# A searched issue order replaced by another from pair 12 on, in a kernel of clustered attention and a causal expert layer

## The chip, the cores and the metric

One core of one Trainium2 chip runs the whole program in one launch. The metric is the device time of one execution in microseconds, given as the median of several runs; smaller is better. Engines are called PE (TensorE), DVE (VectorE), ACT (ScalarE), POOL (GpSimd) and SP (SyncE, which here only issues transfers).

## The reference

Two parts follow each other. Clustered attention: 4 batches of 8 heads, 768 positions, head size 64; every q and k row is assigned to the nearest of 16 centroids of its head, and a query sees only the keys of its own cluster. The result, heads side by side, is the input of an expert layer: 4 experts, each with causal attention of its own (head size 64), of which every position uses two, weighted by its gate.

```python
mask = q_assign[:, :, :, None] == k_assign[:, :, None, :]
scores = np.where(mask, scale * np.matmul(q, k.transpose(0, 1, 3, 2)), -1000000000.0)
attn = softmax(scores)                      # rows, with 1e-9 in the divisor
x = (attn @ v).transpose(0, 2, 1, 3).reshape(B, S, H * D)
logits = x @ w_gate                         # the two largest of 4, softmax over them: w
for e in range(E):
    a = softmax(causal(scale * (x @ wq[e]) @ (x @ wk[e]).T))
    out += (chosen e) * w * (a @ (x @ wv[e]) @ wo[e])
```

## The kernel before, in words

Work goes in head pairs, since two heads of 64 fill the 128 partitions. Pairs 0 to 15 are the clustered attention, pairs 16 to 23 the experts (four batches, two pairs of experts each). The function `core(n)` does a pair's attention, in two halves of 384 queries. It makes the scores twice: once with queries on the partitions, to find each row's maximum (L873 for attention, L877 for the experts; DVE masks and reduces at L886 and L888), and once with keys on the partitions (L960), with the maximum subtracted by additional contraction rows, so that ACT can apply the exponential (L966) straight into `p`. The row maxima travel to those rows `tk` by a small SBUF transfer from `tm`. POOL sets the causal zeros (L971). L1004 multiplies `p` with the values.

The divisors are sums over keys. The exponentials are first added up across key blocks into `acc` (helper `sum_op`: L326 on POOL or L327 on DVE), and one visit of PE, `total` (L1044), sums over the partitions. The sums go through `ssb` (L1048 on ACT or L1051 on DVE), to DRAM (`sd`), back in another layout (`r`, L1067 takes the reciprocal; with the gate's weights `g` at L1069), to DRAM again (`rd`) and back as a broadcast (`rb`), with which the product is normalised (L1095 for attention, an L326 or L327 into `avu` for the experts, followed by a split into a rounded part, `xk` or `kt`, and its rest, `xq` or `qt`). The last pair does without that way through DRAM: `last_half` sums with one-column matmuls (L790, L792) and broadcasts with small ones (L805).

The experts' q and k projections are L666 and L675, their values L706, the gate L712 to L755, the output projection L1133: three matmuls for every 128 rows and every pair, whose result ACT or DVE copies out of PSUM for the transfer to `out_dram`. A transfer is always issued by SP, in the order in which SP meets it (helper `dma`, L311), and a waiting transfer holds up those behind it.

No program order sets what is issued when. The code builds a `Plan` of 2499 steps, and each step may hold several instructions. Two tables written out in the file replay a search that was made beforehand: `ORDER` lists the steps as they are issued (`34` is step 34; a `*` makes it take its other engine, as ACT or DVE for a copy and POOL or DVE for an addition; `~8` puts in 8 filler matmuls), and `SLOTS` gives the slot of each buffer, among them 642 uses of the four double banks of PSUM (`pp`). `Plan.run` checks that no step comes ahead of one that it needs, and then calls them in turn. An instruction waits on the chip only for what it needs and for the former users of its slots.

```python
for step in ORDER.split():
    ...
    other = step[-1] == "*"
    o = self.ops[int(step.rstrip("*"))]
    ...
    list(o.ways.values())[other][1]()
```

Of the kernel before, what the change touches and what calls it, by code (L numbers as in the profile page):

```python
# [35 lines left out]
0 19 ~34 1 4 2 31 ~7 5 8 7 56 6 11* 9 3 10 32 12 ~17 20 13* 16* 33 21 55 22 54 35 34 ~13 60 14 147 39 18* 23 61 17* 24  # L36
62* 15* ~21 25 148 29 28* 41* 27 30* ~8 70 74 71 68 36 75 80 38 242 72 69 37 78 73 57 79 59 76 58 87 77 63 93 335 85
40 81 94 82 42* 88 83 44 84 86 64 91 241 105 92 100 106 45 114 101 46 108 115 102 109 47 95 103 111 96 104 89 112 117
90 97 66* 98 150 99 243 107 430 48 49 118 121 51 52* 110 53 244 162 50 133 122 163 336 158 134 113 119 159 160 120 127
161 156 116 128 166 43 157 130 167 124 131 123 164 125 136 165 146 168 169 65* 338 170 137 138 561 126 188 145 139 152  # L40
129 177 186 189 140 178 171 187 191 132 172 141 175 200 192 176 142 173 201 135 197 174 179 198 181 144 180 194 190
143 182 195 203 183 154* 184 149 185 151 193 655 196 222 204 213 258 223 537 254 259 219 205 199 255 260 547 220 216
261 560 252 153* 217 214 253 250 215 256 251 225 218 257 228 226 548 275 229 262 231 276 221 245 263 246 232 264 233
224 67 206 234 227 337 294 240 155 271 235 295 202 282 272 236 269 265 283 237 285 230 266 429 280 286 270 288 281
247* 273 289 291 274 267 292 239 207 284 297 268 238 277 278 248* 279 431 432 748 287 308 307 290 298* 367 309 354 368
536 310 538 355 350 311 293 319 208 351 299 352 320 313 353 312 348 314 209 346 349 316 347 344 317 315 322 345 323
325 356 357 318 326 358 327 211 535 300 328 321 550 329 374 334* 296 330 361 388 375 331 362 359 551 389 210 376 360
654 363 324 377 379 364 365 380 369 366 382 340 370 385 332 339 342* 333 301 383 562 386 391 371 372 378 563 373 302
341 437 381 402 401 392* 444 403 384 413 303 445 438 414 416 439 842 541 440 387 417 404 441 448 405 446 449 410 390
447 442 411 407 443 406 408 419 450 451 420 452 305 421 409 393 422 412 423 470 249 428* 461 656 471 482 304 462 459  # L50
483 468 415 394 460 424 479 306 469 425 463 473 480 549 418 464 457 474 453 458 476 434 472 454 455 427 477 485 426
456 475 465 466 395 467 436* 936 478 498 486 495* 579 499 577 580 496 396 481 749 578 594 497 507 595 543 573 508 484
501 574 539 575 502 569 576 397 510 500 570 571 511 504 487 572 433 503 505 513 581 582 514 552 583 515 540* 506 488
516 399 517 599 343 522* 509 518 590 607 600 591 584 608 542* 604 585 519 398 586 605 489 601 587 512 588 602 592 589
613 565 521 593 610 603 490 520 611 596 597 614 616 598 567 545 751 606 564 843 657 435 609 638 617 212 626 673 491
639 665 544* 674 629 612 666 669 1031 630 627 670 671 628 632 672 554 663 631 633 667 664 641 668 635 642 492 684 636
675 644 634 658 645 659 676 646 615 677 493 647 637 685 701 648 698 702 653* 640 680 699 693 681 649 678 695 694 679
650 643 688 618 696 686 689 707 566* 687 682 651 704 619 683 652 705 697 690 845 708 710 691 750 692 660* 620 568 700
721 711 720 759 722 621 661* 723 760 937 761 724 729 762 763 725 730 726 764 757 727 767 1030 758 703 735 768 765 736
# [12 lines left out]
1028 1062 1056 524 1063 1075 1086 905 1027 1035 1057 942* 1066 1067 1068 1076* 906 1037* 1087 1154 1139 1096 1155 1088  # L72
1102 526 1140 1133 1079 1103 1097 1132 1134 1135 1098 1099 1136 559* 1143 1100 1082 1111 1144 998 1141 1112 1158 1142
1108 523 1101 1159 1137 1109 1105 1138 1085 1106 1114 1145 1146 1115 1147 1104 1116 1117 1107 1118 1174 1123 944 1127
553* 1177 1175 1000 1168 1178 1110* 1156 1119 1163 1169 1157 1113 1120 1171 1164 1150 1148 1172 1151 1165 1036* 1129
1121 1149 1152 1122 1166 1180 1153 999 1160 1161 1167 1126 1162 1219 555* 1170* 1190 1229 1173 1181 1233 1230 1193
1234 1566 1235 1194 1191 1089 1131* 1236 1218 1227 1192 1196 1228 1237 1195 1197 1231 1202 1232 1199 1203 1238 1176
1205 1567 1239 1240 1200 1241 1198 1128 1206 1208 1221 1209 1223 1090 1179 1210 1091 529 1182 1201 1211 1092 1259 1217
1038 1262 533* 1260 1212 1204 1248 1263 1271 1249 1242 1272 1268 1207 1243 1213 1252 1257 1269 1253 1214 1130* 1246
1001 1258 1250 1247 1265 1251 1244 1215 1266 1261 1274 1216 1245 1183 1220 1093 1254 1222 1255 1094 1256 1568 1312  # L80
1264* 1284 1321 1275 1336 1267 1322 1296 1337 1323 1297 1285 1276 1324 1270 1327 1286 1313 1287 1184 1328 1329 1288
1290 1225* 1330 1325 1291 1331 1326 1293 1185 1289 1332 1342 1294 1299 1333 1300 1302 1292* 1334 1295 1343 1335 1303
1304 1186 1224* 1362 1311 1305 1320 1273 1346 1363 1351 1306 1347 1338 1298 1352 1353 1277 1339 1307 1359 907 1354
# [5 lines left out]
1432 1577 1440 1433 1453 1582* 1318* 1434 1579* 1435 1580 1583 1443 1370 1446 1466 1454 1463 1455 1483 1467 1475 1449
1484 1095 1493 1283 1476 1464 1494 1456 1319* 1491 1572 1465 1478 1492 1485 1479 1469 1486 1468 1487 1470 1472 1488  # L90
1489 1473 1504 1471* 1500 1592 1490 1474 1495 1496 1590 1505 1497 1452 1587 1371 1593 1372 1501 1373 1584 1374 1481
1588 1591 1589 1585* 1586 1625 1515 1626 1521 1516 1482* 1498 1522 1513 1499 1506 1514 1524 1507 1508 1517 1525 1518
# [1117 lines left out]
```

## Time and profile before

| | |
|---|---|
| median of 3 runs | 647.41 us |
| the runs | 646.45, 647.41, 649.11 us |
| span of the profiled execution | 644.0 us |
| its own time | not recorded apart; the median is 3.4 us above the span |
| mean granted clock of PE | 0.997 of full |
| PE busy | 634.8 us, 99% |
| DVE, POOL, ACT busy | 484.6, 466.9, 302.5 us |

The span runs from the first to the last instruction of the profiled execution; the time of a run also holds what lies before and after it. A PE that is busy all the time is the bound whatever the others do, so the table by stretch, the chain and the timelines of single engines are what tells a change of order apart.

### The profile page before, as it was taken

To read this page: it belongs to the slowest core of one execution; us is meant where nothing else is said; L and a number is where in the kernel's file an instruction comes from. 1 tells how busy PE (TensorE), PEld (TensorE's weight loads), DVE (VectorE), ACT (ScalarE), POOL (GpSimd) and SP (SyncE) were. 2 spreads that over 40 slices of the span, in tenths; PEclk is the share of its full clock that TensorE was granted. 3 is DMA by queue.
4 is the path that set the end of the run, shared out by engine and by line. 5 is a ranking of instruction groups with operands and counts; after the bars stand their busy time and mean duration, and the time that the engine had idled before them with its cause. 6 is when DMAs were issued, how large, how long until landed. Compare 5 with 4: busy or idle time off the path is not lost.

```text
span 644.0 us, 13775 instructions
## 1 busy us (share of the span) xinstructions
PE 634.8 (99%) x5404; PEld 482.6 (75%) x5404; DVE 484.6 (75%) x813; ACT 302.5 (47%) x499; POOL 466.9 (72%) x337
## 2 busy tenths in 40 slices
PE   8999999999999999999999999999999999999997
PEld 7667677676776666767757787879879879878775
DVE  5987888798787786888989656574885696678843
ACT  4756546466464654646556323342342423244523
POOL 4399999999999999999999937763754476122500
PEclk9999999999999999999999999999999999999989
DMA  9654445445253323425542310311321220021223
GB/s 192 106 93 95 112 97 113 102 101 106 56 121 99 93 60 86 128 70 107 119 125 75 102 57 2 99 52 51 100 75 28 75 78 24 21 83 68 85 93 131
DMA packets 128119, 55.99 MB, mean 87 GB/s; under 512 B 109820, under 2 KB 117688, under 8 KB 128056
## 3 DMA queue, kind: packets, MB, share of 16 engines
q1 hardware_dynamic: 126488, 54.74, 33.8%
q8 instruction: 42, 0.69, 0.5%
q10 hardware_dynamic: 1568, 0.39, 0.3%
q14 instruction: 21, 0.17, 0.1%
HBM read 39.29 MB, written 15.67 MB: 85 GB/s over the span
## 4 chain that ended last, share of the span: by engine, by line
PE 79%; POOL 14%; issue 2%; DVE 2%; ACT 1%; DMA 0%; SPq 0%; POOLq 0%; ACTq 0%; DVEq 0%
PE pp L960 22%; PE pp L1004 20%; PE pp L666 11%; POOL acc L326 10%; PE pp L873 7%; PE pp L1133 6%; PE pp L706 5%; PE pp L1044 2%; PE pp L877 2%; POOL xt L1095 2%; DVE mx L888 1%; PE pp L522 1%; POOL tk L326 1%; PE pp L1148 1%; POOL tq L326 1%
## 5 line engine op out<-in xcount | busy, mean ns | idle before, releaser
L326 POOL TENSOR_TENSOR acc<-acc,p 128x768 f32<-128x768 f32 (+2 forms) x143 | 249.2, 1752 | 42.0 <-DVE acc L327 38.0
L888 DVE TENSOR_REDUCE mx<-pp 128x2 f32<-128x768 f32 (+1 forms) x224 | 204.2, 943 | 47.8 <-PE pp L873 37.1
L966 ACT ACTIVATE p<-pp 128x768 f32<-128x768 f32 (+2 forms) x264 | 196.8, 773 | 78.4 <-PE pp L960 71.6
L960 PE MATMUL pp<-tq,tk 64*128 64x384 f32 (+2 forms) x1584 | 180.1, 333 | 0.8 <-ACT p L966 0.6
L960 PEld LDWEIGHTS pp<-tq,tk 64*128 64x128 f32 x1584 | 135.7, 186 | 20.7 <-issue 11.9
L1004 PE MATMUL pp<-p,vt 128*64 128x384 f32 x768 | 130.9, 491 | 0.0
L1004 PEld LDWEIGHTS pp<-p,vt 128*64 128x64 f32 x768 | 52.4, 137 | 75.9 <-issue 69.0
L326 POOL TENSOR_TENSOR acc<-p,p 128x768 f32<-128x768 f32 (+1 forms) x41 | 74.3, 1813 | 19.8 <-ACT p L966 18.0
L960 PE MATMUL pp<-tk 49*128 49x384 f32 (+2 forms) x528 | 88.3, 329 | 0.0
L873 PE MATMUL pp<-tk,tq 64*128 64x384 f32 x384 | 69.9, 360 | 1.0 <-ACT ssb L1048 0.7
L873 PE MATMUL pp<-tk 48*128 48x384 f32 x384 | 65.7, 338 | 0.0
L971 POOL TENSOR_SCALAR_AFFINE_SELECT p<-p 128x256 f32<-128x256 f32 x48 | 20.5, 443 | 54.6 <-ACT p L966 53.9
L873 PEld LDWEIGHTS pp<-tk,tq 64*128 64x128 f32 x384 | 48.4, 248 | 6.8 <-issue 2.1
L960 PEld LDWEIGHTS pp<-tk 49*128 49x128 f32 x528 | 50.3, 185 | 0.0
L873 PEld LDWEIGHTS pp<-tk 48*128 48x128 f32 x384 | 49.1, 252 | 0.1
L321 ACT ACTIVATE avu<-pp 128x384 f32<-128x384 f32 x32 | 15.7, 490 | 70.9 <-PE pp L1004 57.1
L886 DVE TENSOR_TENSOR pp<-pp,tri 128x256 f32<-128x256 f32 x48 | 20.6, 428 | 26.5 <-PE pp L877 23.1
L1004 PE MATMUL pp<-p,vm 128*64 128x384 f32 (+2 forms) x288 | 39.6, 420 | 0.0
L1095 POOL TENSOR_TENSOR xt<-avu,rb 128x384 f32<-128x384 f32 x24 | 29.7, 1277 | 11.0 <-DMA rb<-rd 11.0
L1004 PEld LDWEIGHTS pp<-p,vm 128*64 128x64 f32 x288 | 19.3, 137 | 22.6 <-issue 17.9
L327 DVE TENSOR_TENSOR acc<-acc,p 128x768 f32<-128x768 f32 (+2 forms) x23 | 24.7, 1072 | 7.5 <-POOL acc L326 7.5
L706 PE MATMUL pp<-wvh,xh 128*128 128x260 f32 x96 | 27.5, 287 | 0.0
(212 smaller groups left out, 993.5 us busy)
## 6 DMA issues: line engine op xcount, KB each, us to landing
rb<-rd SPq DMA_DIRECT2D x46, 192.0 KB
x<-xt SPq DMA_DIRECT2D x16, 384.0 KB
out_dram<-xt SPq DMA_DIRECT2D x21, 256.0 KB
vt<-in_v_dram SPq DMA_DIRECT2D x52, 96.0 KB
vt<-x SPq DMA_DIRECT2D x12, 384.0 KB
kt<-in_k_dram SPq DMA_DIRECT2D x28, 96.0 KB
qt<-in_q_dram SPq DMA_DIRECT2D x28, 96.0 KB
rw<-rows SPq DMA_DIRECT2D x14, 192.0 KB
```

What stands on the lines that cost most here:

```text
L326: ways = [("pool", t_pool(n), lambda: POOL.tensor_tensor(dst(), a(), b(), op=fn)), ("dve", t_dve(n), lambda: DVE.tensor_tensor(dst(), a(), ...
L327: ("dve", t_dve(n), lambda: DVE.tensor_tensor(dst(), a(), b(), op=fn))]
L666: PE.matmul(m()[:, hf, :HW], w_[:, dc, es], x_[dc]()[:, c], start=(i == 0), stop=(i == 3 * DC - 1))
L706: PE.matmul(m()[:, c % 2, :NV], x_[dc]()[:, ts], w_[:, dc, :], start=(i == 0), stop=(i == 3 * DC - 1))
L873: PE.matmul(ps()[:, h, :HW], at, kt[rs, i * HW:(i + 1) * HW], start=(j == 0), stop=(j == 1))
L886: DVE.tensor_tensor(e, e, tri[:, None, :].to_broadcast([128, 2, 128]), op=OP.add)
L888: DVE.tensor_reduce(to, ps()[:, :, :w], axis=AX.X, op=OP.max)
L960: PE.matmul(to, kt[rs, kc * 128:(kc + 1) * 128], by, start=(i == 0), stop=(i == 3))
L966: ACT.activation(pt()[:, :, o_:HW], p()[:, :, o_:HW], AF.Exp, scale=SC)
L1004: PE.matmul(av()[h * 64:(h + 1) * 64, 0, o_:HW], d["vv"](h, kc), pt()[:, h, o_:HW], start=(kc == 0), stop=(kc == nk - 1), tile_position=(0 ...
L1095: e.tensor_tensor(xt().rearrange("d (j u f c) -> d f c u j", j=32, u=4, f=2)[:, par], avu()[:, c].rearrange("d (c u j) -> d c u j", c=HC, ...
L1133: PE.matmul(m()[:, c % 2], a_()[:, ts], w_()[:, ep, :], start=(ep == 0 and i == 0), stop=(ep == EP - 1 and i == 2))
```

## The change

Only the tables `ORDER` and `SLOTS` are replaced. The plan's steps, their code and their instructions stay as they are; a step may take its other engine.

```diff
@@ -33,121 +33,121 @@
 ORDER = """
-0 19 ~34 1 4 2 31 ~7 5 8 7 56 6 11* 9 3 10 32 12 ~17 20 13* 16* 33 21 55 22 54 35 34 ~13 60 14 147 39 18* 23 61 17* 24
...
+4 19 0 ~34 1 2 31 ~7 5 8 56 7 6 11* 9 3 10 32 12 13* ~17 20 16* 21 55 54 22 33 147 ~13 60 23 35 34 14 24 39 18* 62*
...
 SLOTS = """
-0123131012302132213130202120103332000331312211201122200333130300321312110023102221312303203310223022110220033031211331
...
+0123131002302032213131202021113332010331332211200012121333032200313221320012301113231202102320133011230110033032122312
...
```

The table's first lines differ as well, but there only steps of different engines stand in another order among each other, which no engine sees: every engine keeps its rows up to about 322.7 us of the trace, the second half of pair 12. Behind it 109 steps take their other engine: 36 additions or subtractions go from POOL to DVE and 22 from DVE to POOL, one product of L1095 goes from DVE to POOL, 23 copies go from ACT to DVE and 23 from DVE to ACT, and four more steps (`ssb` among them), two each way. POOL has 13 instructions fewer, DVE 13 more. PE has the same matmuls in another order. Of the 642 uses of PSUM banks 439 have another slot, also in the half whose order is the same, and some 60 buffers in SBUF have.

SP's queue at the place where the orders part, around 320 to 326 us. `rd`, `rb`, `r` and `sd` belong to the divisors, `vt` is loaded values, `x` and `vm` the expert layer's input, and `tk` from `tm` the row maxima of pair 13. Before:

```order
L311 DMA rd<-r_4416 128x12
L311 DMA tk_95<-tm_4591 1x4x96 x2
L311 DMA rb_4602<-rd 64x768 x2
L311 DMA vt_4619<-in_v_dram 32x2x384 x4
L311 DMA r_4661<-sd 128x12
L311 DMA x_107<-xt_3773 128x768
```

After:

```order
L311 DMA rd<-r_4416 128x12
L311 DMA vm_4550<-x_103 128x768
L311 DMA x_107<-xt_3757 128x768
L311 DMA r_4572<-sd 128x12
L311 DMA rb_4595<-rd 64x768 x2
L311 DMA tk_95<-tm_4602 1x4x96 x2
```

The maxima's transfer has moved from behind `rd` to behind `rd`, two moves of `x`, `r` and `rb`.

The divisors of pair 22, near 609 to 623 us. On ACT before, where `xk` is the rounded part of the pair ahead and `p` are exponentials:

```order
L321 ACTIVATE xk_8193<-avu_7714 128x768
L966 ACTIVATE p_0_8195<-pp_8127 128x2x256
L1048 ACTIVATE ssb_8204<-pp_8175,eps 128x384
L966 ACTIVATE p_0_8206<-pp_8149 128x768
L743 ACTIVATE gs_7901<-gs_7901 128x6
L321 ACTIVATE avu_8221<-pp_8175 128x384
```

On DVE after:

```order
L327 TENSOR_TENSOR avu_7693<-avu_7693,rb_8085 128x768
L322 CAST xk_8195<-avu_7693 128x768
L327 TENSOR_TENSOR xq_8211<-avu_7693,xk_8195 128x768
L327 TENSOR_TENSOR acc_0_8213<-p_0_8193,p_0_8209 128x768
L1051 TENSOR_SCALAR ssb_8218<-pp_8197 128x384
L322 COPY avu_8220<-pp_8197 128x384
L327 TENSOR_TENSOR acc_0_8213<-acc_0_8213,p_0_8186 128x768
```

`ssb` has gone from ACT (L1048) to DVE (L1051), and now follows the normalisation of the pair ahead.

SP's queue for the same pair, with the gate's transfers `gd` and `g` and the outputs between. Before:

```order
L311 DMA sd<-ssb_8204 4x384
L311 DMA out_dram<-xt_8230 128x512
L311 DMA r_8249<-sd 128x12
L311 DMA gd_8251<-gr_8245 24x128
L311 DMA out_dram<-xt_8247 128x512
L311 DMA g_8265<-gd_8251 128x12
L311 DMA rd<-r_8249 128x12
L311 DMA out_dram<-xt_8282 128x512
L311 DMA out_dram<-xt_8296 128x512
L311 DMA rb_8304<-rd 64x768 x2
```

After:

```order
L311 DMA sd<-ssb_8218 4x384
L311 DMA out_dram<-xt_8230 128x512
L311 DMA gd_8241<-gr_8236 24x128
L311 DMA out_dram<-xt_8251 128x512
L311 DMA r_8254<-sd 128x12
L311 DMA g_8257<-gd_8241 128x12
L311 DMA g_8268<-gd_8241 128x12
L311 DMA rd<-r_8254 128x12
L311 DMA out_dram<-xt_8287 128x512
L311 DMA rb_8302<-rd 64x768 x2
```

The read of `r` has moved behind `gd` and a second output; `rb` stands at the same distance from `sd`.

PE near the end, from 620.7 us on: the last pair's one-column sums and the output projection (`s` and `rows` are the slots that hold the two parts of the weights). Before:

```order
L790 MATMUL pp_8291<-ones_85,acc_0_8191 128x1
L792 MATMUL pp_8291<-ones_85,p_0_8270 128x1
L790 MATMUL pp_8291<-ones_85,acc_0_8191 128x1
L792 MATMUL pp_8291<-ones_85,p_0_8270 128x1
L790 MATMUL pp_8298<-ones_85,acc_0_8189 128x1
L792 MATMUL pp_8298<-ones_85,p_0_8122 128x1
L790 MATMUL pp_8298<-ones_85,acc_0_8189 128x1
L792 MATMUL pp_8298<-ones_85,p_0_8122 128x1
L790 MATMUL pp_8298<-ones_85,acc_0_8189 128x1 x2
L790 MATMUL pp_8291<-ones_85,acc_0_8191 128x1 x4
L1133 MATMUL pp_8313<-s_5460,kt_8098 128x512
L1133 MATMUL pp_8313<-rows_5467,kt_8098 128x512
```

After:

```order
L790 MATMUL pp_8280<-ones_85,acc_0_8233 128x1
L792 MATMUL pp_8280<-ones_85,p_0_8183 128x1
L790 MATMUL pp_8280<-ones_85,acc_0_8233 128x1
L792 MATMUL pp_8280<-ones_85,p_0_8183 128x1
L790 MATMUL pp_8292<-ones_85,acc_0_8213 128x1
L792 MATMUL pp_8292<-ones_85,p_0_8270 128x1
L790 MATMUL pp_8292<-ones_85,acc_0_8213 128x1
L792 MATMUL pp_8292<-ones_85,p_0_8270 128x1
L1133 MATMUL pp_8189<-s_5092,kt_8073 128x512
L1133 MATMUL pp_8189<-rows_5461,kt_8073 128x512
L1133 MATMUL pp_8189<-s_5092,qt_8082 128x512
L790 MATMUL pp_8280<-ones_85,acc_0_8233 128x1 x2
```

The L1133 group stands ahead of the last one-column matmuls now, which follow in three pieces, each behind three L1133.

## Rows read from the trace of the kernel before

**Rows 1.** The page's busy line: busy us, share, instructions of each engine

```profile
PE 634.8 (99%) x5404; PEld 482.6 (75%) x5404; DVE 484.6 (75%) x813; ACT 302.5 (47%) x499; POOL 466.9 (72%) x337
```

**Rows 2.** Stretches: length, busy us per engine (PE, PEld, DVE, ACT, POOL), PEclk, DMA, GB/s

```profile
317.00:644.00 327.00, 323.08 (x2604) 261.23 (x2604) 225.62 (x426) 126.45 (x243) 174.64 (x151) 0.99 0.23 72
620.00:623.00 3.00, 3.00 (x25) 2.55 (x23) 1.76 (x3) 0.00 (x1) 0.00 (x0) 1.00 0.39 137
624.00:627.00 3.00, 3.00 (x10) 2.42 (x10) 0.52 (x3) 0.00 (x0) 0.00 (x0) 0.50 0.30 94
```

**Rows 3.** The chain that ended last, behind 322: start us, us, work

```profile
323.58 4.02 PE pp L1004 x24
327.61 0.90 PE pp L960 x8
...
412.13 2.31 PE pp L666 x12
...
439.74 2.10 PE pp L666 x12
...
631.63 8.56 PE pp L1133 x36
640.25 0.60 ACT xt L321
```

**Rows 4.** Timeline of PE, 606 to 644: start us, length, engine, line, operands

```profile
609.67 0.85 PE L1044 MATMUL pp<-acc,ones 128*32 128x384 f32 x8
...
620.71 0.35 PE L790 MATMUL pp<-ones,acc 128*128 128x1 f32 x2
...
622.48 1.65 PE L790 MATMUL pp<-ones,acc 128*128 128x1 f32 x12
623.99 0.78 PE L1133 MATMUL pp<-s,kt 128*128 128x512 f32 x1
...
626.70 0.68 PE L790 MATMUL pp<-ones,acc 128*128 128x1 f32 x4
627.24 0.48 PE L1133 MATMUL pp<-s,xk 128*128 128x512 f32 x1
...
631.56 0.50 PE L1133 MATMUL pp<-s,kt 128*128 128x512 f32 x1
```

**Rows 5.** Timeline of the other engines and SP's queue, 612 to 632

```profile
612.07 0.58 ACT L1048 ACTIVATE ssb<-pp,eps 128x384 f32<-128x384 f32 x1
...
615.35 0.38 SPq L311 DMA_DIRECT2D r<-sd  x1
...
622.22 1.10 SPq L311 DMA_DIRECT2D rb<-rd  x2
...
627.92 0.95 DVE L327 TENSOR_TENSOR avu<-avu,rb 128x768 f32<-128x768 f32 x1
...
629.50 0.96 DVE L327 TENSOR_TENSOR qt<-avu,kt 128x768 fp32r<-128x768 f32 x1
```

**Rows 6.** Timeline at the seam: the row maxima of pair 13

```profile
323.87 0.44 DVE L923 STREAM_TRANSPOSE tm<-M 128x192 f32<-128x192 f32 x1
...
324.34 1.16 SPq L311 DMA_DIRECT2D tk<-tm  x2
...
325.60 1.17 SPq L311 DMA_DIRECT2D rb<-rd  x2
```

**Rows 7.** Additions into acc by engine: ns min/median/max, first and last start

```profile
L327 DVE TENSOR_TENSOR acc<-acc,p x23: 414/957/2496, 233.1 to 619.9; 128x768 f32<-128x768 f32 x18, 128x512 f32<-128x512 f32 x3, 128x256 f32<-128x256 f32 x2
L326 POOL TENSOR_TENSOR acc<-acc,p x143: 727/1842/2548, 33.5 to 607.5; 128x768 f32<-128x768 f32 x126, 128x256 f32<-128x256 f32 x12, 128x512 f32<-128x512 f32 x5
```

**Rows 8.** Timeline around 313: an addition beside two POOL products

```profile
312.24 3.52 POOL L1095 TENSOR_TENSOR xt<-avu,rb 128x384 f32<-128x384 f32 x2
...
313.01 1.76 DVE L327 TENSOR_TENSOR acc<-acc,p 128x768 f32<-128x768 f32 x1
```

**Rows 9.** Timeline around 607: the last addition of POOL into acc

```profile
607.49 0.73 POOL L326 TENSOR_TENSOR acc<-acc,p 128x256 f32<-128x256 f32 x1 [3.86 <-DVE acc L327]
```

More of the change, by code (lines that the diff above doesn't have):

```diff
@@ L89 @@
[L89 to L92, printed above, removed]
-1509 1527 1519 1376* 1502 1528 1633 1600 1503 1477 1510 1511 1692 1601 1573* 1512 1480* 1634 1574* 1695 1520 1457 1458
@@ new lines @@
+732 766 752 728 769 753 770 771 733 738 739 740 706 494 712 741 731 747 801 742 772 709 743 787 773 802 744 782 622
+788 774 734 789 775 795 790 783 745 792 746 796 737 713 776 793 778 777 798 755* 780 779 799 804 781 791 784 785 939
+786 938 623 714 624 805 815 794 625 814 859 715 816 817 860 855 818 754* 820 856 861 821 716 851 862 829 556 797 558
+853 852 806 830 826 400 854 823 827 819 857 824 832 858 800 863 864 833 865 834 822 662 835 803 883 841* 874 836 884
+889 825 875 837 872 866 890 873 838 881 756 717 867 892 882 886 893 828 868 839 887 870 807 869 895 847 840 831 876
@@ new lines @@
+1451 1436 1424 1562* 1438 1437 1421 1439 1431 1422 1444 1401 1392 1429 1317 1402 1581 1445 1319 1281 1430 1395 1404
+1578 1403 1432 1433 1316* 1453 1579 1573 1580 1582 1434 1372 1583 1373 1318 1435 1440* 1443* 1374 1454 1463* 1466 1320
+1504 1467 1475 1505 1487 1476 1478 1455 1488 1506 1479 1464 1507 1489 1465 1472 1490 1468 1483 1473 1469 1484 1491
+1470 1493 1575* 1485 1471 1494 1584 1446* 1587 1486 1449 1492 1592 1376* 1375 1577 1377 1590 1456 1691 1474 1481 1593
+1588 1585 1589 1591 1495 1477 1496 1586 1497 1480 1482 1635 1508 1636 1500 1515 1452 1501 1524 1516 1509 1513 1525
@@ new lines @@
+1965 1967 1962 2077 1980 1983 1978 1968* 2070 2074 2064 2075 2160 1997 1961 2071 1986* 1989 2154 2161 2162 2065 2157
+2155 2066 2078 1990* 2067 2039 2156 1902 1969 1994* 1898 2158* 2151 2159 1874 1899 2152* 2231* 1903 2153 2232* 1999
+1900 2234* 1904 1905 2239 2040 1901 2235* 2000 2177 2084 2178 1966 2236 2089 2081 2079 2090 2085 2080 2179 2171 2082
+1910 2172 1970 2083 1906 2086 2088 1998 2240 1911 2180 1907 2241* 2167 1908 2110 2168 1912 1909 2107 2111 1913 2117
+2087* 2108 2163 2105 2041 2118 2237* 2121 2164 2106 2238* 2113 2122 2114 2091 2093 2109* 2115 2119 2094 2104* 2175
@@ new lines @@
+2173 2092 2165 2174 2095 2242 2176 2042 2245 2043 2044 2045 2046 2047 2048 2049 2050 2051 1914 2243 2052 2181 2166
+1918 2262 2182 2112* 2183 1971 2169 2116 1915 2244 2170 2246* 1919 2247 2254 2096 2123 1916* 2120 1920* 2264 2124 2251
+2097 1972 2098 2053 2099 2260 2252* 2253 2100 2054 2258 2248 2261 2259 2055 2256 2056 2249 2101* 2057 2263 1973 2250
+2125 2257 2058 2265 2102* 2255 1921 1917 2266 2103 1974 2126 2192 2187 2193 2299 2220 2188 2300 2184 2189 2221 2267
+2289 2216 2268 2185 2290 1975* 2224 2217 2297 2208 2298 2225 2210 2218 2209 2194 2213 2186 2211 2190 2291 2293 2214
@@ L150 @@
-123
+0101010101010110101000000000000000000000000011000110010111110101010101010011010100110110101000101000000000000000010321
+032
 """
```

180 lines of the change are left out of this document (82 added, 98 removed), and 6 rows, old and new, of the table ORDER.

## The prediction

> **What bounds the kernel now.** I read the busy line of the page first [rows 1]: in a span of 644.0 us TensorE is busy 634.8, the other engines at most three quarters. A mean hides stages, so the table by stretch came next, cut where the two programs begin to differ. In the 327 us behind 317 [rows 2] PE is busy 323.1; the missing 3.9 us are the end of the program, where the chain shows the last matmuls ending at 640.2, then one eviction and the output transfer [rows 3]. So from 317 to 640 TensorE never stands, while DVE works 225.6 and POOL 174.6 of the 327 us. The chain that ended last says the same: from 323 on it is a string of PE lines. The reader is to see that only two things can move the end: PE's own matmuls taking another time, or another engine, slack before, now making PE wait.
>
> One stretch of PE is slower than the rest. From 624 to 627 the granted clock is 0.50, which is 1.2 GHz, where 620 to 623 has 1.00 [rows 2]. Ahead of it stands an unbroken run of one-column matmuls, the sums of the last pair (L790, L792), from 620.71 to 623.99; the L1133 matmuls that follow take half as long again, until 627.24 [rows 4].
>
> **The change, part by part.** Up to about 322.7 us (second half of pair 12) every engine keeps its rows. Behind it the same matmuls stand in another order, 109 steps take their other engine, and 439 of 642 PSUM slots are new.
>
> *TensorE's own work.* Counted over both orders behind 322.7, PE changes between its row and column tilings 63 times in each; the kinds differ by a handful. What such a change is worth is seen in two equal projections: 2.31 us for twelve L666 at 412.13, 2.10 us at 439.74 [rows 3], where only the first follows matmuls of another tiling; I call it 0.2 us. A few changes of another kind give 0 to 0.4 us either way; I take 0 here.
>
> *The last pair's sums.* Before, 14 one-column matmuls (28 passes) ran unbroken for 623.99 − 620.71 = 3.28 us [rows 4]. After, the longest run is 8 matmuls (16 passes): by the same rows up to 622.48, 1.77 us; the other 8 stand in twos and fours between L1133 groups. I expect TensorE to stay at the full clock. The stretch at half clock lasts 627.24 − 623.99 = 3.25 us and holds six L1133 and four passes of L790. At full clock an L1133 takes 8.56/36 = 0.238 us [rows 3] and a pass (623.99 − 622.48)/12 = 0.126 us [rows 4]: 6 × 0.238 + 4 × 0.126 = 1.93. Gain 1.3 us, bounds 0 (the clock falls all the same) and 1.3. Each of the three places where the sums are now cut in may cost up to 0.1 us (an allowance; the trace has one such place, at 626.70, and there at half clock). That is part of the next term.
>
> *The sums of pair 22.* Its ssb (L1048 to L1051) moves from ScalarE to VectorE, behind a product, a cast, a difference and an add of the pair before, and SP issues the gate's gd and a second output ahead of the read r. Before: ssb at 612.07, r issued at 615.35, rb at 622.22, the product with rb at 627.92, its rest qt at 629.50 until 630.46, wanted by the L1133 at 631.56 [rows 4, 5]. There are 1.1 us of cover. By the durations of the rows that now stand ahead, ssb is ready some 0.8 us later and r is issued some 0.7 us later; rb was landed before DVE came to it, so most of this is taken up there, and I estimate qt at 630.45. But with the clock at full level PE comes 1.3 us earlier, to 630.3. A stall of 0 to 0.5 us; with the cuts above I take +0.2.
>
> *The seam.* SP's DMA of pair 13's row maxima (tk from tm) stands behind four other transfers now, where one (rd) stood ahead of it in the rows shown. Before it was issued at 324.34, right behind its source, ready at 324.31 [rows 6]; the first L960 that reads it starts at 327.61 [rows 3], 3.27 us later. rb must wait for rd to land, but so it did before (issued at 325.60 [rows 6]); VectorE has one reduction and one transpose more ahead of the source. My estimate of the new issue is 0.6 to 0.8 us later, which leaves 2.5 us. Of what it needs the rows tell only that 3.27 us is enough: if all of it is needed, PE stalls 0.8 us at the most, if 2.5 do, not at all. Bounds 0 and 0.8 us; I take 0, since the row holds two issues over 1.16 us and the second had 2.7 us at most.
>
> *The engines chosen.* 36 additions and subtractions go from POOL to DVE and 22 the other way; 23 copies go from ACT to DVE and 23 back. Of an addition's two prices, 0.957 us on DVE and 1.842 on POOL (medians [rows 7]), DVE gains 14 × 0.96 = 13 us of work and POOL loses 14 × 1.84 = 26. DVE then has 239 of 327 us: covered, so I cost it at 0. What covers it is PE's own work; if the cover is gone, a late sum stops PE at L1044, where the last such add ended 607.49 + 0.73 = 608.22 for an L1044 at 609.67 [rows 9, 4]: 1.45 us of slack.
>
> Here the trace holds something against the change. The DVE add at 313.01 took 1.76 us while POOL ran its two L1095 products, 312.24 to 315.76 [rows 8], against the median of 0.957; the longest took 2.496 [rows 7]. The Trainium skill (SBUF — State Buffer, section "SBUF: two separate sides") says that VectorE and GpSimd share one port pair as an exclusive lock: a VectorE instruction with two SBUF inputs and a GpSimd one that reads SBUF do not overlap, and the loser waits for the whole of it. That add agrees in direction, though it lost 0.8 us and not the whole of POOL's pair. By that rule each of the 36 moved adds could wait for one POOL addition, 36 × 1.84 = 66 us of DVE time, more than hides easily; by the median row it is 13 us, since most of DVE's adds are not stretched. I take the row.
>
> *Slots.* In the half whose order is unchanged, slots are permuted too. Of the few whose earlier owner was released last, the lateness in the trace is at most 0.2 us; ±0.3 us, taken as 0.
>
> **Sum.** −1.3 + 0.2 = −1.1 us, span 642.9. The span of before is 644.0 and the median of its runs 647.4; I take the 3.4 us between them to stay: **646.3 us**.
>
> **The rivals.**
>
> *A: the clock falls all the same.* For it: before the fall PE ran nothing but one-column matmuls, and 16 passes in a row are still there, with more among the L1133 groups. Against it: the run is half as long. Then the gain is 0 and the cost 0 to 0.2: 647.4 to 647.6 us. With a stall of 1 to 2 us at the seam or at pair 22, it is near 649.
>
> *B, slower: VectorE late with the sums.* The place is L1044, ten visits from pair 13 to 22. For it: adds stretched by POOL [rows 7, 8] and slack of 1.45 us at the one visit shown [rows 9]. Two adds in a row stretched from 0.957 to 2.496 come 3.1 us late and stop PE 3.1 − 1.5 = 1.6 us per visit. It passes 0.5% (3.2 us) from three visits on, since 1.1 is won: 4.8 − 1.1 = 3.7; with four it is 6.4 − 1.1 = +5.3, **652.7 us**. Against it: in the rows most DVE adds take 0.957, and POOL now has 26 us less to collide with.
>
> *C, faster by over 0.5%.* Adding up, for every matmul behind 322.7, the least time that its kind took in this trace with the same tiling before it, the last L1133 would start 3.0 us earlier than it does; that includes the half clock, and the rest (1.7) is spread over hundreds of matmuls. All of it plus the slots of the first half (0.3): 647.4 − 3.3 = **644.1 us**. Against it: nothing in the orders says why the small losses should all go.
>
> That the change does nothing at all is rival A without its cost.
>
> **How the numbers follow.** Forecast (clock stays, nothing new waits) 0.53; A 0.21; A with a small new wait, near 649, 0.06; B 0.12; C 0.08. Half a per cent, 3.2 us, is about what a measurement of this kernel can tell from no change: the runs of before alone span 2.7. Forecast and both forms of A lie within: 0.80; faster is C, 0.08; slower is B, 0.12. The range leaves out B and C, 0.20 together, and takes in the bounds of the rest: below, 646.3 less the slots' 0.3 and the spread of a median of three (1.6 us, nearly the 1.7 by which the highest run of before stands above the middle one) gives 644.4; above, 647.6 plus the two waits at their bounds with spread, 0.8 + 0.5 + 0.7, gives 649.6.
>
> **What would show it.** The clock: granted 1.00 in every stretch from 600 to 640, and the six L1133 behind the sums at 0.24 us each. If A holds, a stretch at 0.50 stands behind the one-column matmuls again. The seam: no idle time of PE ahead of the first L960 of pair 13. Pair 22: the L1133 that reads qt starts without waiting for DVE. B: waits of PE at L1044 released by an add, several of them, and DVE adds well over 1 us beside POOL work. C: the PE matmuls behind 323 shorter by line with no change of clock. The forecast is wrong if PE's idle time from 317 to its last matmul is over 1 us, or if the half clock is there again.

## The result, and the profile after

The change made the kernel slower: 652.11 us in the median of 11 runs against 648.48 of 11 runs of before, a ratio of 1.0081 with a 95% interval of 1.0056 to 1.0107. Ratios and intervals, here and below, are taken over all runs; the quotient of these two medians alone is 1.0056. The prediction named 646.3 us and a range up to 649.6; the measured time lies above it.

The runs after the change fall into two groups by their granted clock. Eight of eleven have a span of 648.8 to 651.0 us at a mean clock of 0.996 to 1.000, three of 655.1 or 655.2 at 0.990 or 0.991. The profiled execution is one of the three (span 655.1, time 656.77), so its rows hold a loss that most runs don't have, and this is taken out below.

The busy line of the page answers to [rows 1]; the work moved as the change says, 13 instructions from POOL to DVE:

```profile
PE 640.5 (98%) x5404; PEld 484.1 (74%) x5404; DVE 501.4 (77%) x826; ACT 302.7 (46%) x499; POOL 453.4 (69%) x324
```

The stretches answer to [rows 2] (length, busy us of PE, PEld, DVE, ACT and POOL, then PEclk, DMA, GB/s):

```profile
322.00:620.00 298.00, 293.06 (x2397) 236.12 (x2395) 227.60 (x413) 116.69 (x225) 152.79 (x132) 1.00 0.21 65
620.00:630.00 10.00, 10.00 (x63) 7.29 (x61) 3.07 (x7) 2.06 (x6) 3.45 (x3) 0.98 0.28 90
630.00:640.00 10.00, 10.00 (x40) 6.87 (x40) 2.61 (x9) 1.16 (x2) 0.00 (x0) 0.51 0.24 86
```

Before, PE was busy in all of 317 to 640. Now 4.9 us are missing from 322 to 620 alone, at full clock. From 630 to 640 the clock is 0.51, the lower of the two levels; by their mean clocks, most runs lack that stretch.

The timeline of PE names the missing 4.9 us. These are the rows behind 320 in which PE stood idle, with the idle time and what ended it in brackets:

```profile
333.38 0.51 PE L873 MATMUL pp<-tk,tq 64*128 64x384 f32 x2 [0.84 <-DVE mx L888]
...
461.00 0.44 PE L666 MATMUL pp<-xh,wqh 128*128 128x384 f32 x1 [0.59 <-DVE ssb L1051]
...
483.09 0.45 PE L666 MATMUL pp<-xh,wqh 128*128 128x384 f32 x1 [0.59 <-DVE ssb L1051]
...
485.82 0.42 PE L666 MATMUL pp<-xh,wkh 128*128 128x384 f32 x1 [0.36 <-DVE M L888]
...
514.55 0.44 PE L666 MATMUL pp<-xh,wqh 128*128 128x384 f32 x1 [0.50 <-DVE ssb L1051]
...
542.60 0.44 PE L666 MATMUL pp<-xh,wkh 128*128 128x384 f32 x1 [0.67 <-DVE avu L322]
...
571.36 0.79 PE L960 MATMUL pp<-tq,tk 64*128 64x384 f32 x6 [1.15 <-DVE M L888]
...
602.52 0.79 PE L960 MATMUL pp<-tq,tk 64*128 64x384 f32 x6 [0.22 <-DVE ssb L1051]
```

The sum is 4.92 us, and each wait is ended by an instruction of DVE. Where [rows 3] showed one unbroken string, eight gaps stand now. They are of two kinds.

Five of them (461.00, 483.09, 514.55, 542.60, 602.52; 2.57 us) are of this form (all engines, 459.7 to 461.4):

```profile
459.74 0.67 PE L877 MATMUL pp<-tk,tq 64*128 64x128 f32 x6
459.86 0.49 ACT L321 ACTIVATE avu<-pp 128x384 f32<-128x384 f32 x1 [1.63 <-PE pp L1004]
...
460.38 0.56 DVE L1051 TENSOR_SCALAR ssb<-pp 128x384 f32<-128x384 f32 x1 [0.67 <-ACT avu L321]
...
461.00 0.44 PE L666 MATMUL pp<-xh,wqh 128*128 128x384 f32 x1 [0.59 <-DVE ssb L1051]
```

The double bank that L1044 and L1004 have filled is read by two engines: ACT copies the product, DVE the sums (at 542.60 the other way round). DVE stands for 0.67 us and starts 0.03 us behind the end of ACT's copy (460.35). The trace tells why: `ssb` carries a wait for the semaphore that ACT raises at the end of its copy, though it needs nothing of it. So in this program the second reader of a double bank waits for the first one too, beyond what it needs and the former users of its slots. The next step that takes a bank behind three score steps (L877) is a projection (L666), and it was given this very bank. It stands until the second reader has ended at 460.94. Followed through the tables of before, the same five steps took other banks, whose last reader was not one of this pair of copies and had ended earlier; in the trace of before none of them waits.

The other three (333.38, 485.82, 571.36; 2.35 us) are of this form (DVE and POOL, 568 to 572):

```profile
568.53 1.84 POOL L326 TENSOR_TENSOR avu<-avu,rb 128x768 f32<-128x768 f32 x1
...
568.55 1.85 DVE L735 TENSOR_TENSOR gt<-gt,ramp 128x24 f32<-128x24 f32 x1
...
570.33 0.42 DVE L886 TENSOR_TENSOR pp<-pp,tri 128x256 f32<-128x256 f32 x1
...
570.78 0.43 DVE L888 TENSOR_REDUCE M<-pp 128x2 fp32r<-128x256 f32 x1
...
571.36 0.79 PE L960 MATMUL pp<-tq,tk 64*128 64x384 f32 x6 [1.15 <-DVE M L888]
```

L735 works on 24 columns. It takes 1.85 us, and ends at 570.40 with POOL's product (568.53 + 1.84 = 570.37). Behind it DVE's reduction for the bank that L960 wants is late, and PE stands 1.15 us. At 482.95 L1069 (12 columns) took 1.66 us in the same way, and at 330.08 an addition took 2.38 us while POOL ran the addition of 329.79:

```profile
329.79 1.84 POOL L326 TENSOR_TENSOR acc<-acc,p 128x768 f32<-128x768 f32 x1
...
330.08 2.38 DVE L327 TENSOR_TENSOR acc<-acc,p 128x768 f32<-128x768 f32 x1
...
332.38 0.95 DVE L888 TENSOR_REDUCE mx<-pp 128x2 f32<-128x768 f32 x1
```

POOL was done at 331.63, and 331.63 + 0.957 [rows 7] is 332.59, where the row has 332.46.

A last difference lies behind PE's last matmul. From there to the end of the span it was 3.9 us before (640.17 to 644.03) and is 4.7 now (650.4 to 655.1). The stretches there (columns as above) show the transfer engines full for three microseconds:

```profile
650.00:651.00 1.00, 0.37 (x2) 0.00 (x0) 0.23 (x1) 0.55 (x1) 0.00 (x0) 1.00 1.03 383
651.00:652.00 1.00, 0.00 (x0) 0.00 (x0) 0.00 (x0) 0.05 (x1) 0.00 (x0) 1.00 1.02 375
652.00:653.00 1.00, 0.00 (x0) 0.00 (x0) 0.00 (x0) 0.00 (x0) 0.00 (x0) 1.00 1.05 406
653.00:654.00 1.00, 0.00 (x0) 0.00 (x0) 0.00 (x0) 0.00 (x0) 0.00 (x0) 0.73 0.18 66
```

Three outputs, issued from 650.26 to 651.18, move at the same time; before, the last three were issued at 638.80, 640.13 and 640.88.

### The profile page after: what moved, and what is told of

It is laid out like the page before. It is cut to its first block, busy times and chain, and to the rows that moved or that the text cites. A ratio compares the mean times of both kernels' runs of the same rounds, so it can differ in the third digit from the quotient of the medians.

```text
span 655.1 us, 13774 instructions
## 1 busy us (share of the span) xinstructions
PE 640.5 (98%) x5404; PEld 484.1 (74%) x5404; DVE 501.4 (77%) x826; ACT 302.7 (46%) x499; POOL 453.4 (69%) x324
## 4 chain that ended last, share of the span: by engine, by line
PE 87%; POOL 5%; DVE 3%; ACT 2%; issue 1%; DMA 0%; SPq 0%; ACTq 0%; POOLq 0%; DVEq 0%
PE pp L960 25%; PE pp L1004 23%; PE pp L666 10%; PE pp L873 10%; PE pp L1133 6%; PE pp L706 5%; POOL acc L326 4%; PE pp L1044 3%; PE pp L522 1%; PE pp L877 1%; PE pp L1148 1%; POOL xt L1095 1%; DVE mx L888 1%; PE pp L790 1%; DVE acc L327 0%
## 5 line engine op out<-in xcount | busy, mean ns | idle before, releaser
L326 POOL TENSOR_TENSOR acc<-acc,p 128x768 f32<-128x768 f32 (+2 forms) x134 | 237.6, 1782 | 56.5 <-DVE acc L327 25.4
L888 DVE TENSOR_REDUCE mx<-pp 128x2 f32<-128x768 f32 (+1 forms) x224 | 204.1, 944 | 47.7 <-PE pp L873 33.8
L960 PE MATMUL pp<-tq,tk 64*128 64x384 f32 (+2 forms) x1584 | 180.8, 334 | 2.2 <-DVE M L888 1.2
L960 PEld LDWEIGHTS pp<-tq,tk 64*128 64x128 f32 x1584 | 135.7, 186 | 23.4 <-issue 13.4
L1004 PE MATMUL pp<-p,vt 128*64 128x384 f32 x768 | 130.9, 490 | 0.0
L1004 PEld LDWEIGHTS pp<-p,vt 128*64 128x64 f32 x768 | 52.3, 137 | 75.9 <-issue 67.7
L960 PE MATMUL pp<-tk 49*128 49x384 f32 (+2 forms) x528 | 88.0, 329 | 0.0
L326 POOL TENSOR_TENSOR acc<-p,p 128x768 f32<-128x768 f32 (+1 forms) x38 | 68.5, 1804 | 18.1 <-ACT p L966 18.1
L971 POOL TENSOR_SCALAR_AFFINE_SELECT p<-p 128x256 f32<-128x256 f32 x48 | 24.1, 518 | 49.8 <-ACT p L966 49.6
L960 PEld LDWEIGHTS pp<-tk 49*128 49x128 f32 x528 | 50.0, 185 | 0.0
L1004 PE MATMUL pp<-p,vm 128*64 128x384 f32 (+2 forms) x288 | 40.8, 429 | 0.0
L1004 PEld LDWEIGHTS pp<-p,vm 128*64 128x64 f32 x288 | 19.4, 139 | 23.9 <-issue 19.6
L327 DVE TENSOR_TENSOR acc<-acc,p 128x768 f32<-128x768 f32 (+2 forms) x32 | 32.4, 1018 | 4.8 <-POOL acc L326 3.7
L1095 POOL TENSOR_TENSOR xt<-avu,rb 128x384 f32<-128x384 f32 x25 | 31.3, 1281 | 2.3 <-DMA rb<-rd 2.2
L326 POOL TENSOR_TENSOR xl<-vt,xh 128x768 fp32r<-128x768 f32 x9 | 16.7, 1859 | 16.1 <-DVE xh L322 13.8
```

What stands on the lines that cost most here:

```text
L326: ways = [("pool", t_pool(n), lambda: POOL.tensor_tensor(dst(), a(), b(), op=fn)), ("dve", t_dve(n), lambda: DVE.tensor_tensor(dst(), a(), ...
L327: ("dve", t_dve(n), lambda: DVE.tensor_tensor(dst(), a(), b(), op=fn))]
L888: DVE.tensor_reduce(to, ps()[:, :, :w], axis=AX.X, op=OP.max)
L960: PE.matmul(to, kt[rs, kc * 128:(kc + 1) * 128], by, start=(i == 0), stop=(i == 3))
L971: POOL.affine_select(out=c, in_=c, pattern=[[0, 2], [1, 128]], compare_op=OP.is_ge, fill=0.0, base=0, channel_multiplier=-1)
L1004: PE.matmul(av()[h * 64:(h + 1) * 64, 0, o_:HW], d["vv"](h, kc), pt()[:, h, o_:HW], start=(kc == 0), stop=(kc == nk - 1), tile_position=(0 ...
```

## The experiments

Two theories stood at the start. Theory 1: the loss is the eight waits, through banks handed on too early and through DVE instructions held up by POOL. Theory 2: DVE as a whole is overloaded by the work that was moved to it.

**How steady is the kernel before.** `before_again` is the kernel before, unchanged.

> The kernel before, unchanged, to see how its span and its granted clock vary from run to run. If the half-clock stretch of 3.25 us in the profiled execution is in every run, the clock is 0.997 in each and the spans lie within 1 us of 644.0. If it varies as after the change (0.990 to 1.000 there), the spans differ by several us with the clock. Ratio 1.000 either way.

Ratio 1.0017 (0.9996 to 1.0039). The second case held: 12 runs with spans from 642.5 us at a clock of 1.000 to 648.2 at 0.993. Its profile (647.2) shows a wait that the first one did not have:

```profile
621.37 0.17 DVE L1069 TENSOR_TENSOR r<-r,g 128x12 f32<-128x12 f32 x1 [1.56 <-DMA g<-gd]
621.46 0.68 DVE L327 TENSOR_TENSOR acc<-acc,p 128x512 f32<-128x512 f32 x1
...
622.29 0.35 PE L790 MATMUL pp<-ones,acc 128*128 128x1 f32 x2 [1.08 <-DVE acc L327]
...
627.25 0.77 PE L1133 MATMUL pp<-s,kt 128*128 128x512 f32 x1
```

L1069 waits for the gate's transfer, the additions into acc stand behind it on DVE, and the last sums stand behind those on PE. In the first profile L1069 waited 0.44 us, and PE not at all. So the execution profiled for the prediction was one of the quicker ones: two other runs of before with its span of 644.0 took 645.7 and 646.0 us, some 2.5 less than the median.

**Choices apart from order.** Both tables were split: one kernel has the order and slots of before and only the 109 stars of after, the other has the reverse.

```diff
 # order_before_engines_after: ORDER and SLOTS of before, for each step that changed engine
-1301
+1301*
...
 # order_after_engines_before: ORDER and SLOTS of after
-1301*
+1301
...
```

> The order and slots of before, with the 109 engine choices of after. Theory 1 (single waits: banks handed on too early by the new order and slots, and a few instructions of DVE blocked by POOL at certain places): the banks are handed on as before, so no wait at the projections; blocked instructions fall elsewhere, 0 to 2 us of waits; ratio 1.000 to 1.003. Theory 2 (DVE is overloaded by the work that moved to it): the 5 us come along, ratio 1.006 to 1.010.

> The order and slots of after, with the engine choices of before. Theory 1: the waits for banks at L666 stay (2.6 us in all), the two blocked places whose instructions had changed engine (332.5 and 570.2, together 2.0 us) go, others may come; ratio 1.003 to 1.007. Theory 2: the loss goes with the choices, ratio 0.998 to 1.002.

Measured: 1.0222 (1.0192 to 1.0251) and 1.0208 (1.0173 to 1.0242). Neither theory named this. The loss does not go along with the choices, since taking them back makes it worse; this speaks against theory 2, which `sums_unread` below decides. Theory 1 put both kernels too low. The order and the choices were searched together, and each is worse with the other's partner: the two hybrids have 7.6 and 8.1 us of PE waits behind their first 320 us. Those of the first hybrid are at other places than after, such as these two (timeline of PE):

```profile
337.73 1.27 PE L1044 MATMUL pp<-acc,ones 128*32 128x384 f32 x8 [1.85 <-DVE mx L888]
...
619.72 0.80 PE L960 MATMUL pp<-tq,tk 64*128 64x384 f32 x6 [1.94 <-DVE avu L322]
```

In the second hybrid, which has the slots of after, four of the five waits for a bank are still there (0.58, 0.59, 0.52 and 0.61 us at L666), as theory 1 said; in the first one, with the slots of before, none of them is:

```profile
464.55 0.44 PE L666 MATMUL pp<-xh,wqh 128*128 128x384 f32 x1 [0.58 <-DVE ssb L1051]
...
487.52 0.44 PE L666 MATMUL pp<-xh,wqh 128*128 128x384 f32 x1 [0.59 <-DVE ssb L1051]
```

**The late reader of the bank.** `sums_unread` makes five of the 23 `ssb` from a constant, so that one of the two reads of the bank falls away. The divisors of these five pairs are left out of the computation.

```diff
 def finish(o, m):
+    ones = ones32[:, 0:1].to_broadcast([128, HW])
-        ACT.activation(ssb(), m()[:, 1, :HW], AF.Identity, bias=eps)
+        ACT.activation(ssb(), ones if n == 19 else m()[:, 1, :HW], AF.Identity, bias=eps)
-        DVE.tensor_scalar(ssb(), m()[:, 1, :HW], EPS, None, op0=OP.add)
+        DVE.tensor_scalar(ssb(), ones if n in (16, 17, 18, 21) else m()[:, 1, :HW], EPS, None, op0=OP.add)
```

> The kernel after, where the five ssb (pairs 16 to 19 and 21) that are read out of the bank in turn with the copy avu are made from a constant instead of the sums: the same engines and order, but the bank is free once avu is copied, about 0.55 us earlier. This leaves out these five reads, so the outputs are wrong there. Theory 1: the waits of PE at 460.4, 482.5, 514.1, 541.9 and 602.3 (0.59, 0.59, 0.50, 0.67, 0.22) fall to under 0.1 each, 2.4 us less; the waits at 332.5, 485.5 and 570.2 stay. Theory 2 (DVE overloaded): no change, since DVE has the same work.

647.12 us, ratio to before 1.0007 (0.9981 to 1.0033), 5 us less than after. One wait of PE is left behind 320:

```profile
333.13 0.51 PE L873 MATMUL pp<-tk,tq 64*128 64x384 f32 x2 [0.82 <-DVE mx L888]
```

The five are gone as theory 1 said, and theory 2 falls: DVE was not relieved, since its four `ssb` from the constant took 0.35, 0.43, 0.55 and 1.74 us, where each took 0.56 in after. The two at 485.5 and 570.2 are gone too, which theory 1 did not say, so the gain is twice its 2.4 us: L735 and L1069 no longer met a long POOL instruction. L735 took 0.185 us at the most, the L1069 of that place 0.36. Whether that is because PE is earlier, or because DVE no longer stands ahead of these `ssb` (0.56 us at 482.47 in after), was not told apart.

**The held-up instructions.** `locks` changes three steps of after: the addition of 330.08 (step 1301) and the product of 568.53 (1975) on their engines of before, and L1069 (1742) behind two reductions.

```diff
-1354 1301* 1308
+1354 1301 1308
-1936 1742 1886 1866 2022 1937 1880 1743 1935 2013
+1936 1886 1866 2022 1937 1880 1935 1742 1743 2013
-2290 1975* 2224
+2290 1975 2224
```

> The kernel after with three steps set otherwise: the addition at 330.08 back on POOL, the product with rb at 568.53 back on DVE, and L1069 (482.95) behind the two reductions that stood behind it. Theory 1 (a DVE instruction with two SBUF inputs waits for the whole POOL instruction): L1069 takes 0.2 us instead of 1.66, L735 0.2 instead of 1.85, the waits of PE at 332.5, 485.5 and 570.2 (0.84, 0.36, 1.15) go, 2.35 us less; the five others stay. If those were only queueing on DVE, the durations stay long and the waits move.

650.71 us, ratio 1.0047 (1.0025 to 1.0069). DVE's timeline at the place of L735:

```profile
568.15 0.18 DVE L735 TENSOR_TENSOR gt<-gt,ramp 128x24 f32<-128x24 f32 x1
...
568.94 0.43 DVE L888 TENSOR_REDUCE M<-pp 128x2 fp32r<-128x256 f32 x1
...
569.28 0.95 DVE L327 TENSOR_TENSOR avu<-avu,rb 128x768 f32<-128x768 f32 x1
```

L735 takes 0.18 us, the reduction behind it ends 1.8 us earlier than in after, and the wait is gone; L1069 took 0.16. The two waits at 485.5 and 570.2 went, the one at 332.5 came back as 0.72 us at L1044 (334.39), since on POOL the addition was late itself. So 4.92 us of waits became 3.27, 1.65 less where 2.35 were expected, and the five of the banks stayed at 0.59, 0.59, 0.49, 0.67 and 0.21.

**Both.** `sums_unread_locks` is the sum of the two edits; the same five divisors are left out.

> Both edits in one kernel (five sums left out as before). Theory 1: the eight waits are the whole of PE's idle time behind 322, so 4.7 us less than after, PE's idle time from 322 to its last matmul under 0.5 us, and the time at that of before within 0.3%. If part of the loss is elsewhere (slower matmuls, clock), that part stays.

647.45 us, ratio 1.0001 (0.9982 to 1.0020): the change's loss against the median of before is gone, 4.7 us as expected. PE's idle time is 0.8 us and not under 0.5, since the wait at L1044 that `locks` brought is here as well (0.72 us). The two causes do not add, since the first edit also removed most of what the second is for. The waits are not the whole difference: runs at a clock of 1.000 have a middle span of 645.6 us here and 642.8 in before, 2.8 more.

**Other banks, nothing left out.** `banks` lets the five steps change places with a score step, so that they take a bank that came free before.

```diff
-1833 1835 1732 1739 1928 1836 1736 1753 1834 1925
+1833 1928 1835 1732 1739 1736 1753 1834 1836 1925
...
-2324 2406 2351 2342 2403
+2324 2342 2406 2351 2403
```

> The kernel after, nothing left out: at the five visits where a projection or score step takes the bank of sums and values right behind its two readers, that step changes places with one score step of the next pair, so that it takes a bank that came free earlier. Theory 1: the five waits (2.6 us) go; TensorE changes its tiling more often (four score steps stand alone between projections, about 0.3 us each by 2.31 against 2.10 at L666 and the like), so 1 to 2 us less than after, ratio to before 1.004 to 1.007. If the late reader itself (DVE) were the bound, the waits move to the displaced score steps and nothing is won.

651.39 us, ratio 1.0078 (1.0046 to 1.0109): no gain that can be told from after, and above the range that was expected. All five waits behind `ssb` or `avu` went, and the one at 571 too. But the projection behind the first place, at 464.78, now waits 1.61 us for the reduction (L888) that reads the bank of the displaced score step, and the wait of 485.82 is still there (0.58 us at 487.21). So at one of the five places the wait passed on to the next reader. And PE's own work grew: 324.5 us in the count given below, the most of all kernels with this order, with 0.8 more at L666 than in `locks`.

**The sums and the clock.** `before_sums_cut` cuts the one-column run of before into pieces of 16, 4, 4, 4 and 4 passes.

```diff
-2363 2431 2437 2468 2467 2368 2470 2364 2436 2369 2439 2365 2432
+2363 2368 2437 2364 2468 2369 2467 2470 2365 2436 2439 2431 2432
```

> The kernel before with only the one-column sums of the last pair cut into pieces between the L1133 groups (longest run 16 passes, then 4, 4, 4 and 4). The prediction's theory: the clock stays at full level, 1.3 us less span, ratio 0.998, clock 1.000 in most runs. Rival: the clock falls all the same, in some runs for longer (after the change 9 us at 0.51 in the profiled run), ratio 1.000 to 1.005.

Ratio 1.0016 (0.9985 to 1.0047), and both cases in one kernel: six of 12 runs at a clock of 0.999 or 1.000 with spans of 643.1 to 645.8, six at 0.989 to 0.992 with 648.0 to 651.3. Of 99 runs of before only one is at 0.992 or below, so where the clock fell here it fell for longer, as the rival said. In its profile PE still stood 1.07 us ahead of the sums. So two more kernels take that wait away, without and with a finer cut (at most eight passes in a row).

```diff
 # adds_ahead
-2360 2429 2460* 2374 2430 2361 2419* 2375
+2360 2460* 2419* 2429 2374 2430 2361 2375
 # adds_ahead_sums_cut, besides
-2469 2362* 2438 2363 2431 2437 2468 2467 2368 2470 2364 2436 2369 2439 2365 2432
+2362* 2431 2363 2468 2368 2467 2369 2469 2470 2364 2437 2436 2365 2438 2439 2432
```

> The kernel before; on VectorE the last two additions into acc stand ahead of L1069 of pair 22, which waits for the gate's transfer g. In the second profile of before that wait was 1.56 us instead of 0.44, and TensorE stood 1.08 us at the last pair's sums behind those additions. If that wait is what makes the runs of before spread, the span falls by about 1 us in most runs, ratio 0.998 to 1.000, and TensorE has no wait at L790; the clock still falls behind the unbroken run of one-column matmuls, 0.995 to 0.997. If the spread is only the clock, nothing changes.

> The same, and the sums cut so that no more than eight passes stand in a row, each piece behind an L1133 group. The prediction's theory of the clock (it falls behind a stretch in which TensorE has little work): clock 0.999 to 1.000 in nearly all runs, span 642 to 643, ratio 0.993 to 0.996, faster than both kernels. Rival: the cut sums keep the clock low for longer in some runs, as in the first kernel with the sums cut (6 of 12 runs at 0.990, 5 us longer): ratio 0.998 to 1.003.

`adds_ahead`: 0.9986 (0.9966 to 1.0006), no wait at L790, but seven of 12 runs with a clock of 0.991 to 0.997. `adds_ahead_sums_cut`: 0.9980 (0.9961 to 0.9999), and all 12 runs at 0.999 or 1.000. So in most runs the clock falls behind the unbroken stretch of one-column matmuls even without the wait, and with that stretch cut up it kept its level in all 12. The ratio is less good than the 0.993 to 0.996 expected: its first L1133 still waited 0.52 us for its bank.

**The last outputs.** `last_outputs` gives the end of after the order and engines of before: the last twelve L1133 steps, with all six evictions on ACT.

> The kernel after, with the last twelve L1133 steps, their evictions and their output transfers in the order and on the engines of before (all six evictions on ACT). After the last matmul the profile of after shows 4.7 us to the end of the span, that of before 3.8; in after the transfer engines are full from 650 to 653, since three outputs start within 0.9 us. Theory: the outputs leave earlier one by one and the end behind the last matmul falls back to 3.8 us, 0.9 us less than after; the waits in the middle stay, ratio to before about 1.006 to 1.008. Rival: the distance is only the latency of the last transfer and stays at 4.7 us.

651.0 us, ratio 1.0041 (1.0027 to 1.0054), below the range expected; all six runs have a clock of 0.999 or 1.000, and none of the 11 runs of before beside them has. Behind its last matmul, at 645.5, the span goes on for 4.0 us instead of 4.7, and the transfer engines are no longer full:

```profile
646.00:648.00 2.00, 0.00 (x0) 0.00 (x0) 0.00 (x0) 0.14 (x1) 0.00 (x0) 1.00 0.70 262
648.00:649.50 1.50, 0.00 (x0) 0.00 (x0) 0.00 (x0) 0.00 (x0) 0.00 (x0) 1.00 0.02 5
```

Part of the gain was given back, since PE now stood 0.84 us ahead of an L1133 at 636.85.

**A version that beats both.** `best_tail` is before with the additions ahead and two pieces of the sums ahead of the first L1133.

```diff
-2469 2362* 2438 2363 2431 2437 2468 2467 2368 2470 2364 2436 2369 2439
+2362* 2431 2363 2468 2467 2368 2437 2436 2364 2469 2470 2369 2438 2439
```

> The kernel before with the two additions ahead of L1069 and the sums cut into pieces of at most eight passes, now with two pieces ahead of the first L1133 that waited 0.52 us for its bank in the kernel with the cut sums. Theory: no wait of TensorE left behind 317, clock 1.000 in nearly all runs, span 642.2 to 643.0, median 644.2 to 645.0, ratio 0.994 to 0.997. Rival: the clock is decided by the first pieces in a row and falls again in part of the runs, ratio 0.998 to 1.000.

644.59 us, ratio 0.9947 (0.9931 to 0.9962), all six runs at a clock of 1.000, where the 11 runs of before beside them have 0.993 to 0.997. PE does not wait behind 317. Its stretches, against [rows 2]:

```profile
317.00:640.00 323.00, 321.18 (x2604) 259.74 (x2600) 225.38 (x426) 126.27 (x243) 174.29 (x151) 1.00 0.23 72
...
620.00:630.00 10.00, 9.95 (x83) 8.29 (x82) 4.75 (x13) 1.08 (x2) 0.00 (x0) 1.00 0.42 146
630.00:642.10 12.10, 8.28 (x36) 6.39 (x34) 2.17 (x5) 4.64 (x8) 0.00 (x0) 1.00 0.35 131
```

The half clock of 624 to 627 is gone, and PE is busy until 638.3.

## Why the prediction was wrong

By its own sign the forecast was wrong: PE's idle time between 317 and its last matmul was to stay under 1 us and was 4.9.

*Where it failed first: "DVE then has 239 of 327 us: covered, so I cost it at 0".* The sum came near (242.3 us of DVE behind 317 in after), but a mean says nothing on single instructions. The prediction had the fact in hand, the stretched addition at 313.01 [rows 8], and put it aside with "I take the row", meaning the median of all additions. It also misread that row, which holds two products of POOL. Alone, the first is (timeline of POOL, before):

```profile
312.24 1.84 POOL L1095 TENSOR_TENSOR xt<-avu,rb 128x384 f32<-128x384 f32 x1
```

It ended at 314.08; the addition ended at 314.77, which less 0.957 is 313.81. So it had waited for nearly the whole of the first product. In after, L735 took 1.85 us in place of 0.18 and ended within 0.03 us of POOL's product. Both agree, to 0.3 us, with the rule that was quoted from the Trainium skill (SBUF — State Buffer, section "SBUF: two separate sides"): the loser waits for the whole POOL instruction.

Nor did the moved additions bring more such meetings. Between 322 and 620 us, some 13 DVE instructions with two SBUF inputs were stretched by over 0.15 us beside POOL in before, and 13 in after, by 7.1 and 10.7 us in all. In before none of them made PE wait, these two among them (timeline of DVE, before):

```profile
517.45 1.11 DVE L734 TENSOR_TENSOR gt<-lg,gs 128x24 f32<-128x24 f32 x1
...
519.71 1.03 DVE L735 TENSOR_TENSOR gt<-gt,ramp 128x24 f32<-128x24 f32 x1
```

In after three of the 13 stand in front of a reduction that PE needs, and cost it 2.35 us. Two of the three are instructions of a few columns that the prediction had not listed. What counts is the place, not the work moved.

*Where it failed second: "Slots ... ±0.3 us, taken as 0".* It followed the banks only in the half whose order is unchanged. Behind it, five steps got the bank that was read last, by two engines in turn: 2.57 us, which `sums_unread` took away.

*Rival B had the right engine and the wrong place.* It put DVE's lateness at L1044, as late sums. None of the eight waits stood there; they stood at the banks of score and projection steps, where DVE is a reader. That its price for four visits, 6.4 us, is near the 4.9 that came, and its 652.7 us near the measured 652.11, is luck.

*"I take 0" for PE's own work.* PE's busy time from the first score step behind 316 to its last matmul, all at full clock, was 321.83 us in `before_sums_cut` and 323.63 in `locks`:

```profile
318.98:642.00 323.02, 321.83 (x2604) 260.12 (x2604) 225.44 (x427) 126.14 (x242) 174.86 (x151) 1.00 0.23 71
...
317.02:644.00 326.98, 323.63 (x2604) 260.50 (x2604) 239.49 (x440) 126.17 (x242) 161.06 (x138) 1.00 0.23 69
```

That is 1.8 us more, of which 0.7 at L1044 came with the wait that `locks` brought there. By other profiles at full clock it is 1 to 2 us, without `banks`: 321.6 and 321.8 with the order of before (`best_tail`, `adds_ahead_sums_cut`), 322.8 and 323.8 with that of after (`sums_unread`, `last_outputs`). In each of them 0.8 to 1.0 of it lies at L960, which is left for another line 64 times instead of 60. No run tested this; the equal count of 63 changes was too coarse.

*The end.* It was not priced at all. It gave 0.8 us away; `last_outputs` won 0.7 of them back.

*The clock was right in kind, and its 1.3 us is too small for the runs.* Most runs after the change do keep the full clock, as forecast, and the stretch at the lower level in the first profile is worth some 1.5 us (PE's busy time is 323.3 there, 321.6 to 321.8 with that order at full clock). But the runs of before lose more than that profile showed: 16 of the 99 runs of before that were taken beside the experiments have a clock of 1.000, with spans of 642.1 to 645.0, and the median span of all is 646.4. And it is not safe: three of 11 runs after the change, at clocks of 0.990 or 0.991, have spans 4.8 us longer (655.1 against 650.3); the profiled one has 10 us at the lower level.

*"I take the 3.4 us between them to stay".* No run shows such a distance between its own span and its own time: it is 1.7 to 3.0 us in runs of before, 2.0 in the middle, and 1.7 to 1.8 in those of after. The 3.4 set a quick execution against a middle one.

*The seam was right, and pair 22 within its bounds.* No wait stands ahead of the first L960 of pair 13, nor at the L1133 that reads qt, for which 0.2 us had been taken.

*The account.* At a clock of 1.000 the middle span is 642.8 us before (16 runs) and 650.3 after (four), 7.5 us apart: 4.9 waits, 0.8 the end, which leaves 1.8 for PE's own work, inside its 1 to 2. The medians of the times show only 3.6 of it, because most runs of before lose some 3.6 us (646.4 − 642.8) at their end, and most runs of after do not. In the second profile of before that loss is the clock and the wait for the gate's transfer; the other runs of before were not profiled. What stays open is the cause of the 1.8 us, which was only read off, and why the hybrids lose as much as 2%.

## What to carry to other kernels

Where one engine is busy without a gap, any new order of the rest has to be judged bank by bank: for each step of the bound engine, look up who reads its bank last and how soon before, since a mean of busy time cannot show it. A small two-input instruction of VectorE that met a long one of GpSimd took the rest of the long one here, so look at the meetings in front of what the bound engine waits for, not at the microseconds moved nor at the number of meetings. And profile the kernel before more than once: here its end varied by more than the whole forecast.

## What the runs showed of the hardware

Two readers of one double bank on different engines ran one behind the other in every case looked at: seven of DVE's eight `ssb` in after started 0.03 us behind the end of ACT's `avu`. This is the program's own wait on a semaphore, as the trace shows, and not a finding on the banks; what they do when both halves are read at once no run here shows. A vector instruction of 24 columns took 1.85 us beside a POOL product and 0.18 without it. And cutting 28 one-column passes into pieces of at most eight, with the wait ahead of them gone, kept TensorE's clock at 0.999 or 1.000 in 18 of 18 runs, where the kernel before had 1.000 in 16 of 99.
